# Causal widths for the single-pass score and average matmuls of an attention and feed-forward kernel

## Chip, cores and metric

The kernel runs on one core of a Trainium2 chip. The metric is device time in microseconds of one execution; the time before is the median of 3 runs.

## What is computed

Three blocks follow each other: causal attention with a decay bias, a gated feed-forward layer, and a second one that takes the maximum of three products. The shapes are B = 4, H = 8, S = 576, D = 64; 2304 tokens; widths 512 to 2048 to 512, then 512 to 768 (three times) to 512.

```python
scores = scale * q @ k.T                          # per batch and head, 576 x 576
cum = cumsum(max(s, 0)); bias = -(cum[:, None] - cum[None, :])
scores = where(causal, -1e9, scores + min(bias, 0))
attn = exp(scores - scores.max()); attn = attn / (attn.sum() + 1e-9)
x = attn @ v                                      # heads side by side: 2304 x 512
h = x @ w_in;  x = (h * clip(h + 3, 0, 6) / 6) @ w_out
h = max(max(x @ w1, x @ w2), x @ w3);  out = h @ w_out2
```

## The kernel before

**A list scheduler writes the order.** The kernel's Python code is a set of generators ("threads"). Each yields either an event, a buffer from a stock, or a request for an engine with a cost in microseconds, as `yield "PE", 2 * mm(n - z)`. The class Flow (L111 to L196) plays these out in modelled time: an engine that is free takes the request of the lowest rank, and the instruction is issued right behind the yield. So the order on each engine, and that of the DMAs, all issued on SyncE's queue, follows from the costs. The cost of a matmul of n columns is `mm(n) = n / 2400 + 0.003` (L199). At run time each engine follows its list in order, and semaphores do the rest.

**Precision.** Float32 operands are split into a rounded high part and the rest, both of the type fp32r; a product is then three single-pass matmuls (high by high, high by low, low by high; `three`, L448 to L452). Batch 0 differs: its averages, and the scores of its first pair of heads, run on plain float32 operands in four passes, which the trace shows as two records for each instruction.

**Attention.** A head's 576 queries come in 5 chunks (c = 0 to 4, the last with 64 queries). `slot` (L764) does one chunk: scores into a PSUM bank, two matmuls for each part (the second one carries the rows of the bias, 66 of them), then the masked minimum on VectorE (L800), exp on ScalarE (L808), the scaling by 1/sum on GpSimd (L346), transposes by TensorE (L849), and a copy of the transposed chunk into a tile et (high part by ScalarE, low part by VectorE, L858). Causality asks for w = (c + 1) * 128 key columns; chunk 4 takes its 576 in two parts of 288. L773 takes `max(w, 256)`, so chunk 0 computes 256 columns where it needs 128; what lies behind w is never read.

`average` (L864) multiplies the transposed weights by the values. A head's chunks form two groups: g = 0 holds queries 0 to 255 and key blocks 0 and 1, g = 1 queries 256 to 575 and key blocks 0 to 4. For batches 1 to 3, each key block x takes two matmuls (high and low part of the weights) whose stationary operand holds both parts of the values side by side (128 columns). L887 sets the first query column: 0 for x up to 2, otherwise n - 256. So key block 1 of group 0 has 256 columns, and key blocks 3 and 4 of group 1 have 256 of 320. Of these, the query columns that lie ahead of the key block are zero. `real_et` (L538) makes the two fp32r tiles for batches 1 to 3 when batch 0 has left the space, and fills these blocks with zeros once (L552, L554, L555), on GpSimd, since no later instruction writes there.

**The feed-forward layers** fill TensorE between the attention's pieces. `hidden1` and `reduce1` run the first layer in two rounds (z = 0 with 6 of 16 column blocks beside the attention, z = 1 behind it), 288 tokens at a time, as 288-column triples. Then `form` (L1099) makes linear combinations of the last layers' weights for a seven-product scheme and stores 10 of 12 in DRAM, `hidden2` computes the three products and their maximum, and `reduce2` the last product. `form` takes its buffers from the stock W of 12: one for the raw weights, then, after decoding, four more (three where it shares one).

Of the kernel before, what the change touches and what calls it, by code (L numbers as in the profile page):

```python
# [198 lines left out]
def mm(n):  # L199
    return n / 2400.0 + 0.003  # L200
# [60 lines left out]
def attn_moe_moe2(ctx, tc, q, k, v, s, w_in, w_out, w1, w2, w3, w_out2, out):  # L261
# [9 lines left out]
    def stock(items=()):  # L271
        return Stock(flow, items)
# [265 lines left out]
    def real_et():  # L538
        yield heads[0, NPAIR - 1, 1].full[1]
        for item, to in lent:  # L540
            if to is DIAG:
                to.move(item, GT)
        DIAG.move((ap, "up0"), UP)
        for g in range(2):
            yield ET[g].get()
            yield ET[g].get()
            shape = [P, 2, 2, 256] if g == 0 else [P, 2, NCH, 320]
            et[1, g] = t = ap.tile(shape, F32R, tag=f"e{g + 1}", name=f"e{g + 1}", bufs=1)
            flat = t.bitcast(F32)
            yield "POOL", 0.5  # L550
            if g == 0:
                pool.memset(flat[:, :, 1, 0:128], 0.0)  # L552
            else:
                pool.memset(flat[:, :, 3, 64:128], 0.0)  # L554
                pool.memset(flat[:, :, 4, 64:256], 0.0)  # L555
            ET[g] = stock([0])
            et_real[g].set()

# [205 lines left out]
    def slot(i, item, tiny):  # L764
        b, p, j, c = seq[i]
        h, pr = heads[b, p, j], pair[b, p]
        passes = yield h.ready
        n = min(P, S - c * P)
        qs = slice(c * P, c * P + n)
        w = min(S, (c + 1) * P)  # L770
        wp = (w + P - 1) // P * P
        e = et[0, "e4"] if c == NCH - 1 else make(item, [P, 512], F32, "e")
        cuts = [(0, 288), (288, 576)] if w > 512 else [(0, max(w, 256))]  # L773
        parts = []
        for lo, hi in cuts:
            bank = yield S_.get()
            ps = make(bank, [P, 512], F32, "ps_s")
            o = ps[:n, 0:hi - lo]
            if (b, p) == (0, 0):
                yield "PE", len(passes) * 4 * mm(min(hi, w) - lo), False, i - AHEAD  # L780
                o, hi = ps[:n, 0:min(hi, w) - lo], min(hi, w)
            else:
                yield "PE", 2 * mm(hi - lo), False, i - AHEAD
            for x, (lhs, rhs) in enumerate(passes):
                pe.matmul(  # L785
                    o, lhsT=lhs[:, qs], rhs=rhs[:, lo:hi],
                    start=(x == 0), stop=(x == len(passes) - 1),
                )
            parts.append((bank, ps, lo, min(hi, w)))
        h.scored += 1  # L790
        if h.scored == NCH:
            for st, it in h.release:
                st.put(it)
        small = make((ap, f"tiny{tiny}"), [P, 4], F32, "tiny")
        m0 = 3.0e38
        shift = (NCH - 1 - c) * P
        for x, (bank, ps, lo, hi) in enumerate(parts):
            m = small[:n, x:x + 1]
            yield "DVE", dve2(hi - lo)
            vec.tensor_tensor_reduce(  # L800
                out=e[:n, lo:hi], in0=ps[:n, 0:hi - lo], in1=above[:n, shift + lo:shift + hi],
                scale=-0.125, scalar=m0, op0=ALU.add, op1=ALU.min, accum_out=m,
            )
            S_.put(bank)
            m0 = m
        r = small[:n, 2:3]
        yield "ACT", act1(w) + 0.186
        act.activation(  # L808
            e[:n, :w], e[:n, :w], AF.Exp, bias=m0, scale=-1.0, accum_out=r,
        )  # L810
        yield "DVE", 0.07
        vec.tensor_scalar(out=r, in0=r, scalar1=1e-9, scalar2=None, op0=ALU.add)
        yield "DVE", 0.075
        vec.reciprocal(r, r)  # L814
        spread = b == 0 and c in DIAGC
        if spread:
            z = yield DIAG.get()
            diag = make(z, [P, P], F32, "diag")
            e_ = yield [(x, COST["scale"][x](P)) for x in ON["diag"]]
            if e_ == "ACT":  # L820
                act.activation(diag[:n, :n], ident[:n, :n], AF.Copy, scale=r)
            else:
                (pool if e_ == "POOL" else vec).tensor_scalar(
                    out=diag[:n, :n], in0=ident[:n, :n], scalar1=r, scalar2=1.0,
                    op0=ALU.mult, op1=ALU.mult,
                )
        else:
            yield from scaled(e[:n, :w], r, w, ON["norm", b == 0])
        TINY.put(tiny)
        g = 0 if c < 2 else 1  # L830
        if b > 0:
            yield et_real[g]
        if c in (0, 2):
            x = yield ET[g].get()
            h.et[g] = (x, et[min(b, 1), g])
            h.claimed[g].set()
        else:
            yield h.claimed[g]
        x, dst = h.et[g]
        o = (c if g == 0 else c - 2) * P  # L840
        bank = yield T.get()
        pt = make(bank, [P, c + 1, n], F32, "pt")
        yield "PE", (4 if spread else 2) * mm(n) * (c + 1)
        for y in range(c + 1):
            cut = e[:n, y * P:(y + 1) * P]
            if spread:
                pe.matmul(pt[:, y, :], lhsT=cut, rhs=diag[:n, :n], start=True, stop=True)
            else:
                pe.transpose(pt[:, y, :], cut, ident[:n, :n])  # L849
        if spread:  # L850
            DIAG.put(z)
        (E4 if c == NCH - 1 else E).put(item)
        dh = dst[:, x, 0:c + 1, o:o + n]
        yield from drained(dh, pt, n * (c + 1), ON["eh", b == 0])
        if b > 0:
            dl = dst[:, 1, 0:c + 1, o:o + n]
            yield "DVE", dve2(n * (c + 1))
            vec.tensor_tensor(out=dl, in0=pt, in1=dh.bitcast(F32), op=ALU.subtract)  # L858
        T.put(bank)
        h.count[g] += 1  # L860
        if h.count[g] == (2 if g == 0 else 3):
            h.full[g].set()

    def average(b, p, j, g):  # L864
        h, pr = heads[b, p, j], pair[b, p]
        if (j, g) == (0, 0):
            xi = yield X32.get()
            pr.x32.set((make(xi, [P, S], F32, "x32"), xi))
        x32, _ = yield pr.x32
        yield h.full[g]  # L870
        vhl = yield h.v
        nj, o, n = GROUP[g]
        y, src = h.et[g]
        bank = yield V.get()
        px = make(bank, [P, 512], F32, "px")
        xo = x32[j * D:(j + 1) * D, o:o + n]
        for x in range(nj):
            last = x == nj - 1
            if b == 0:
                z = max(0, x * P - o)  # L880
                yield "PE", 4 * mm(n - z), not last
                pe.matmul(
                    px[0:D, z:n], lhsT=vhl[:, x, j], rhs=src[:, y, x, z:n],
                    start=(x == 0), stop=last,
                )
            else:
                z = n - 256 if x > 2 else 0  # L887
                yield "PE", 2 * mm(n - z), not last
                for hl in range(2):
                    pe.matmul(  # L890
                        px[:, z:n], lhsT=vhl[:, x, j].rearrange("p l d -> p (l d)"),
                        rhs=src[:, hl, x, z:n], start=(x + hl == 0),
                        stop=(last and hl == 1),
                    )
        ET[g].put(y)
        pr.used += 1
        if pr.used == 4:
            pr.vrelease[0].put(pr.vrelease[1])
        if b == 0:
            yield from drained(xo, px[0:D, 0:n], n, ON["xo"])  # L900
        else:
            ui = yield UP.get()
            up = make(ui, [D, 320], F32, "up")
            yield from drained(up[:, 0:n], px[D:P, 0:n], n, ON["up"])
            yield "DVE", dve2(n)
            vec.tensor_tensor(out=xo, in0=px[0:D, 0:n], in1=up[:, 0:n], op=ALU.add)
            UP.put(ui)
        V.put(bank)
        pr.count += 1
        if pr.count == 4:  # L910
            pr.done.set()
# [180 lines left out]
    def forms_by_name(n, made, single):  # L1092
# [3 lines left out]
            "11": t3[:, 0], "12": t3[:, 1], "22": single,  # L1096
        }

    def form(n):  # L1099
        ri = yield W.get()  # L1100
        r = make(ri, [P, 2, 512], F32R, "wr")
        for half in range(2):
# [7 lines left out]
        if n == 1:  # L1110
            spare, both = yield shared
        else:
            spare = yield W.get()
            both = make(spare, [P, 2, 2, HK], F32R, "wg")
            if n == 0:
                shared.set((spare, both))
        single = both[:, n % 2]
        am = yield AM.get()
        y = make(am[0], [P, HK], F32, "ws")
# [555 lines left out]
```

## Time and profile before

| | |
|---|---|
| time, median of 3 runs | 948.64 us (944.84 to 956.93) |
| profiled execution, span from first to last instruction | 947.3 us |
| TensorE busy in it | 912.1 us, 6460 matmuls |
| up to 125 us: TensorE busy, granted clock | 102.7 us of 125, 0.80 |
| 125 to 350 us | 218.0 us of 225, 0.99 |
| 350 to 666 us | 315.6 us of 316, 1.00 |
| 666 to 947 us | 275.8 us of 281, 1.00 |

How to read it: the trace has one record for each instruction and engine. TensorE has two rows, PE for the matmuls and PEld for the loads of their stationary operand; both overlap among neighbours, since matmuls are pipelined and their ends are modelled, so the cost of one is read from the distance between two starts and not from its length. A form such as `128*64 128x288` means 128 rows by 64 weight columns, and 128 rows by 288 streamed columns. The granted clock is the share of TensorE's full speed that the throttle let through; 1.00 is its level of 2.4 GHz, 0.5 that of 1.2 GHz. A bracket at a row's end is the engine's idle time ahead of it and who ended it.

### The profile page before, as it was taken

What the parts mean: (1) busy time and instruction counts of PE and PEld (TensorE: products, weight loads), DVE (VectorE), ACT (ScalarE), POOL (GpSimd) and SP (SyncE); (2) the same over time, 40 slices, a digit from 0 to 9 for tenths busy, and PEclk for the clock granted to TensorE, in tenths of its full rate; (3) what the DMA queues carried; (4) which work ended last, traced back from release to release, by engine and by line L of the source; (5) the groups of instructions that cost most, each with busy time, mean ns of one, the idle gap of its engine ahead of it and who ended that gap; (6) DMA issues with size and microseconds to landing.
All of it is one profiled execution on the core that took longest, in us unless ns stands there. A gap on an engine that the chain in (4) does not pass through costs nothing.

```text
span 947.3 us, 19211 instructions
## 1 busy us (share of the span) xinstructions
PE 912.1 (96%) x6460; PEld 855.2 (90%) x6460; DVE 738.8 (78%) x2126; ACT 483.3 (51%) x1225; POOL 240.7 (25%) x323
## 2 busy tenths in 40 slices
PE   9887789999999999999999999999999999999998
PEld 5454379988999999999999999999999999999998
DVE  5788779898988943999687889896757666677994
ACT  3575458786887754566444445454223232333552
POOL 4776667666765432310000000000000000000000
PEclk7798779999999999999999999999999999999999
DMA  5799678688876424666449758978762130283542
GB/s 178 170 241 238 177 201 207 186 231 215 213 203 182 125 89 158 201 200 208 129 133 341 272 191 293 308 263 277 275 203 63 39 88 26 75 309 98 158 147 75
DMA packets 97273, 174.96 MB, mean 185 GB/s; under 512 B 10620, under 2 KB 59772, under 8 KB 97176
## 3 DMA queue, kind: packets, MB, share of 16 engines
q1 hardware_dynamic: 97176, 173.75, 60.7%
q8 instruction: 51, 0.84, 0.4%
q14 instruction: 46, 0.38, 0.1%
HBM read 97.99 MB, written 49.17 MB: 155 GB/s over the span
## 4 chain that ended last, share of the span: by engine, by line
PE 73%; DMA 10%; DVE 7%; issue 5%; ACT 2%; POOL 2%; SPq 1%; DVEq 0%; POOLq 0%; ACTq 0%
PE ps_j L451 7%; PE ps_j L452 7%; PE ps_j L450 7%; PE ps_x L452 6%; PE ps_x L450 6%; PE ps_x L451 6%; PE ps_h L450 5%; PE ps_h L451 5%; PE ps_h L452 5%; PE ps_s L785 5%; DMA raw<-in_w_out_dram 3%; PE pt L849 3%; PE px L890 3%; DMA kt<-kb 3%; PE ps_o L451 2%
## 5 line engine op out<-in xcount | busy, mean ns | idle before, releaser
L450 PE MATMUL ps_h<-x,w 128*128 128x288 f32 x512 | 153.3, 299 | 0.0
L450 PE MATMUL ps_x<-gt,w 128*128 128x288 f32 x512 | 151.8, 296 | 0.1
L452 PE MATMUL ps_x<-gt,w 128*128 128x288 f32 x512 | 151.4, 296 | 0.0
L451 PE MATMUL ps_h<-x,w 128*128 128x288 f32 x512 | 151.1, 295 | 0.0
L451 PE MATMUL ps_x<-gt,w 128*128 128x288 f32 x512 | 150.6, 294 | 0.2
L452 PE MATMUL ps_h<-x,w 128*128 128x288 f32 x512 | 150.7, 294 | 0.0
L451 PE MATMUL ps_j<-xf,wf 128*128 128x288 f32 x432 | 127.9, 296 | 0.0
L452 PE MATMUL ps_j<-xf,wf 128*128 128x288 f32 x432 | 127.7, 296 | 0.0
L450 PE MATMUL ps_j<-xf,wf 128*128 128x288 f32 x432 | 127.6, 295 | 0.0
L346 POOL TENSOR_SCALAR e<-e,tiny 128x256 f32<-128x256 f32 (+4 forms) x152 | 101.5, 672 | 82.4 <-DVE tiny L814 25.3
L808 ACT ACTIVATE e<-e,tiny 128x128 f32<-128x128 f32 (+4 forms) x160 | 95.9, 600 | 35.5 <-DVE tiny L800 24.5
L978 ACT ACTIVATE u<-ps_h,half 128x288 f32<-128x288 f32 x128 | 63.6, 497 | 81.4 <-PE ps_h L452 80.6
L785 PE MATMUL ps_s<-kt,qt 66*64 66x288 f32 (+11 forms) x384 | 100.3, 360 | 2.7 <-DVE tiny L800 1.8
L450 PEld LDWEIGHTS ps_x<-gt,w 128*128 128x128 f32 x512 | 96.1, 188 | 1.2 <-DVE g L982 0.4
L450 PEld LDWEIGHTS ps_h<-x,w 128*128 128x128 f32 x512 | 96.1, 188 | 1.0
L451 PEld LDWEIGHTS ps_x<-gt,w 128*128 128x128 f32 x512 | 96.2, 188 | 0.8 <-POOL gt L352 0.7
L452 PEld LDWEIGHTS ps_x<-gt,w 128*128 128x128 f32 x512 | 96.2, 188 | 0.4 <-DVE w L352 0.4
L451 PEld LDWEIGHTS ps_h<-x,w 128*128 128x128 f32 x512 | 96.4, 188 | 0.2
L452 PEld LDWEIGHTS ps_h<-x,w 128*128 128x128 f32 x512 | 96.2, 188 | 0.0
L800 DVE CUSTOM_DVE_ANT_0 e<-ps_s,above 128x128 f32<-128x128 f32 (+4 forms) x160 | 75.0, 474 | 21.6 <-PE ps_s L785 19.7
L849 PE MATMUL pt<-ident,e 128*128 128x128 f32 (+1 forms) x472 | 72.7, 278 | 19.2 <-POOL e L346 13.9
L982 DVE SCALAR_TENSOR_TENSOR g<-u,ps_h 128x288 f32<-128x288 f32 x128 | 57.5, 449 | 41.9 <-ACT u L978 40.9
(160 smaller groups left out, 2169.0 us busy)
## 6 DMA issues: line engine op xcount, KB each, us to landing
x<-x_d SPq DMA_DIRECT2D x64, 288.0 KB
f_d<-wf SPq DMA_DIRECT2D x30, 512.0 KB
wf<-f_d SPq DMA_DIRECT2D x30, 512.0 KB
kt<-kb SPq DMA_DIRECT2D x90, 144.0 KB
raw<-in_w_out_dram SPq DMA_DIRECT2D x22, 512.0 KB
x_d<-xs SPq DMA_DIRECT2D x16, 576.0 KB
raw<-in_w_dram SPq DMA_DIRECT2D x18, 512.0 KB
qt<-qb SPq DMA_DIRECT2D x30, 288.0 KB
```

Source lines behind the costliest of these rows:

```text
L346: (pool if e == "POOL" else vec).tensor_scalar(out=y, in0=y, scalar1=r, scalar2=1.0, op0=ALU.mult, op1=ALU.mult)
L450: pe.matmul(ps, lhsT=wh, rhs=xh, start=first, stop=False, skip_group_check=again)
L451: pe.matmul(ps, lhsT=wh, rhs=xl, start=False, stop=False, skip_group_check=again)
L452: pe.matmul(ps, lhsT=wl, rhs=xh, start=False, stop=last, skip_group_check=again)
L785: pe.matmul(o, lhsT=lhs[:, qs], rhs=rhs[:, lo:hi], start=(x == 0), stop=(x == len(passes) - 1),)
L800: vec.tensor_tensor_reduce(out=e[:n, lo:hi], in0=ps[:n, 0:hi - lo], in1=above[:n, shift + lo:shift + hi], scale=-0.125, scalar=m0, op0=ALU ...
L808: act.activation(e[:n, :w], e[:n, :w], AF.Exp, bias=m0, scale=-1.0, accum_out=r,)
L849: pe.transpose(pt[:, y, :], cut, ident[:n, :n])
L890: pe.matmul(px[:, z:n], lhsT=vhl[:, x, j].rearrange("p l d -> p (l d)"), rhs=src[:, hl, x, z:n], start=(x + hl == 0), stop=(last and hl == 1),
L978: act.activation(ut, ps, AF.Relu, bias=half, scale=1.0 / 6.0)
L982: vec.scalar_tensor_tensor(out=g, in0=ut, scalar=1.0, in1=ps, op0=ALU.min, op1=ALU.mult)
```

## The change

Chunk 0 of the scores computes 128 columns, not 256, for all heads whose scores are single-pass (the first pair had that already). The averages of batches 1 to 3 start at the first query column of their key block: `z = max(0, x * P - o)`. That makes 128 columns of key block 1 in group 0, 192 of key block 3 and 64 of key block 4 in group 1. The zero blocks are then never read, and their memsets and the cost that the scheduler was told for them go. The costs given to the scheduler follow the new widths. Beside it, a stock of three turns lets at most three threads of `form` at a time stand between their start and the moment when they have all buffers.

```diff
--- before.py
+++ after.py
@@ -546,13 +546,6 @@
             yield ET[g].get()
             shape = [P, 2, 2, 256] if g == 0 else [P, 2, NCH, 320]
             et[1, g] = t = ap.tile(shape, F32R, tag=f"e{g + 1}", name=f"e{g + 1}", bufs=1)
-            flat = t.bitcast(F32)
-            yield "POOL", 0.5
-            if g == 0:
-                pool.memset(flat[:, :, 1, 0:128], 0.0)
-            else:
-                pool.memset(flat[:, :, 3, 64:128], 0.0)
-                pool.memset(flat[:, :, 4, 64:256], 0.0)
             ET[g] = stock([0])
             et_real[g].set()
 
@@ -770,15 +763,14 @@
         w = min(S, (c + 1) * P)
         wp = (w + P - 1) // P * P
         e = et[0, "e4"] if c == NCH - 1 else make(item, [P, 512], F32, "e")
-        cuts = [(0, 288), (288, 576)] if w > 512 else [(0, max(w, 256))]
+        cuts = [(0, 288), (288, 576)] if w > 512 else [(0, w)]
         parts = []
         for lo, hi in cuts:
             bank = yield S_.get()
             ps = make(bank, [P, 512], F32, "ps_s")
             o = ps[:n, 0:hi - lo]
             if (b, p) == (0, 0):
-                yield "PE", len(passes) * 4 * mm(min(hi, w) - lo), False, i - AHEAD
-                o, hi = ps[:n, 0:min(hi, w) - lo], min(hi, w)
+                yield "PE", len(passes) * 4 * mm(hi - lo), False, i - AHEAD
             else:
                 yield "PE", 2 * mm(hi - lo), False, i - AHEAD
             for x, (lhs, rhs) in enumerate(passes):
@@ -786,7 +778,7 @@
                     o, lhsT=lhs[:, qs], rhs=rhs[:, lo:hi],
                     start=(x == 0), stop=(x == len(passes) - 1),
                 )
-            parts.append((bank, ps, lo, min(hi, w)))
+            parts.append((bank, ps, lo, hi))
         h.scored += 1
         if h.scored == NCH:
             for st, it in h.release:
@@ -876,15 +868,14 @@
         xo = x32[j * D:(j + 1) * D, o:o + n]
         for x in range(nj):
             last = x == nj - 1
+            z = max(0, x * P - o)
             if b == 0:
-                z = max(0, x * P - o)
                 yield "PE", 4 * mm(n - z), not last
                 pe.matmul(
                     px[0:D, z:n], lhsT=vhl[:, x, j], rhs=src[:, y, x, z:n],
                     start=(x == 0), stop=last,
                 )
             else:
-                z = n - 256 if x > 2 else 0
                 yield "PE", 2 * mm(n - z), not last
                 for hl in range(2):
                     pe.matmul(
@@ -1096,7 +1087,10 @@
             "11": t3[:, 0], "12": t3[:, 1], "22": single,
         }
 
+    FORMING = stock(range(3))
+
     def form(n):
+        turn_ = yield FORMING.get()
         ri = yield W.get()
         r = make(ri, [P, 2, 512], F32R, "wr")
         for half in range(2):
@@ -1114,6 +1108,7 @@
             both = make(spare, [P, 2, 2, HK], F32R, "wg")
             if n == 0:
                 shared.set((spare, both))
+        FORMING.put(turn_)
         single = both[:, n % 2]
         am = yield AM.get()
         y = make(am[0], [P, HK], F32, "ws")
```

## Rows read from the trace of the kernel before

**Rows 1.** The page's head: span, then busy time, share and instructions of each engine.

```profile
span 947.3 us, 19211 instructions
PE 912.1 (96%) x6460; PEld 855.2 (90%) x6460; DVE 738.8 (78%) x2126; ACT 483.3 (51%) x1225; POOL 240.7 (25%) x323
```

**Rows 2.** Windows: stretch, us, busy PE, PEld, DVE, ACT, POOL; granted clock, DMA share, GB/s.

```profile
0.00:125.00 125.00, 102.68 (x423) 60.61 (x423) 90.17 (x305) 65.12 (x170) 83.66 (x103) 0.80 0.80 203
125.00:350.00 225.00, 217.96 (x1602) 206.24 (x1603) 194.10 (x756) 167.93 (x465) 136.48 (x199) 0.99 0.69 184
350.00:666.00 316.00, 315.64 (x2375) 314.11 (x2375) 253.25 (x570) 158.76 (x351) 20.53 (x21) 1.00 0.68 229
```

**Rows 3.** Groups of TensorE's instructions by form: count, busy us, mean ns, idle before.

```profile
L890 PE MATMUL px<-e,vhl 128*128 128x256 f32 x192 | 40.3, 293 | 2.4 <-DVE x L906 1.0 <-DVE tiny L812 0.9
...
L785 PE MATMUL ps_s<-kt,qt 128*128 128x256 f32 x60 | 19.8, 331 | 1.7 <-issue 0.9 <-DVE tiny L800 0.8
```

**Rows 4.** Timeline of TensorE's matmuls: start us, length us, instruction, count.

```profile
212.27 0.40 PE L890 MATMUL px<-e,vhl 128*128 128x256 f32 x2
212.51 0.30 PE L450 MATMUL ps_x<-gt,w 128*128 128x288 f32 x1
212.64 0.29 PE L451 MATMUL ps_x<-gt,w 128*128 128x288 f32 x1
```

**Rows 5.** Weight loads: three rows of the timeline, then two groups by form.

```profile
211.05 0.39 PEld L849 LDWEIGHTS pt<-ident,e 64*128 64x128 f32 x5 [0.29 <-POOL e L346]
211.50 0.19 PEld L450 LDWEIGHTS ps_x<-gt,w 128*128 128x128 f32 x1
211.61 0.19 PEld L451 LDWEIGHTS ps_x<-gt,w 128*128 128x128 f32 x1
...
L785 PEld LDWEIGHTS ps_s<-kt,qt 66*128 66x128 f32 x120 | 23.9, 199 | 0.0
...
L785 PEld LDWEIGHTS ps_s<-kt,qt 66*64 66x64 f32 x60 | 8.7, 145 | 0.3
```

**Rows 6.** Groups of TensorE's instructions by form, from 150 to 346 us alone.

```profile
L450 PE MATMUL ps_h<-x,w 128*128 128x288 f32 x98 | 31.0, 316 | 0.0
L450 PE MATMUL ps_x<-gt,w 128*128 128x288 f32 x99 | 30.4, 307 | 0.0
...
L785 PE MATMUL ps_s<-kt,qt 128*64 128x288 f32 x40 | 12.8, 321 | 0.0
```

**Rows 7.** Timeline of TensorE: batch 0's four-pass averages, two records each.

```profile
69.79 0.54 PE L882 MATMUL px<-e2p,vf 128*64 128x192 f32 x2
70.16 0.38 PE L882 MATMUL px<-e1p,vf 128*64 128x128 f32 x2
70.38 0.28 PE L882 MATMUL px<-e2p,vf 128*64 128x64 f32 x2
```

**Rows 8.** Timeline of GpSimd around the zero fills of the larger tile.

```profile
114.45 0.55 POOL L554 MEMSET e<- 128x128 f32 x1 [5.23 <-PE px L882]
114.95 0.41 POOL L555 MEMSET e<- 128x384 f32 x1
115.34 1.95 POOL L352 TENSOR_TENSOR vhl<-vf,vhl 128x256 fp32r<-128x256 f32 x2
117.25 3.16 POOL L352 TENSOR_TENSOR xs<-x,xs 128x288 fp32r<-128x288 f32 x1
```

**Rows 9.** VectorE's casts of L339 (min/median/max ns, first and last start); then timeline rows.

```profile
L339 DVE CAST vhl<-vf x1: 494/494/494, 114.4 to 114.4; 128x640 fp32r<-128x640 f32 x1
...
115.44 1.00 DVE L339 CAST xs<-x 128x576 fp32r<-128x576 f32 x1
...
121.02 0.69 PE L849 MATMUL pt<-ident,e 128*128 128x128 f32 x2 [5.14 <-POOL e L346]
```

**Rows 10.** Last product of the forming, first load of the next stage, durations as above.

```profile
L352 DVE TENSOR_TENSOR wf<-ws,wf x36: 415/420/432, 490.2 to 651.2; 128x256 fp32r<-128x256 f32 x36
...
L450 PEld LDWEIGHTS ps_j<-xf,wf x432: 187/188/193, 666.0 to 872.8; 128*128 128x128 f32 x144
```

## The prediction

> **What bounds the kernel now.** I read the page first: TensorE is busy 96% of the span, its weight loads 90%, the next engine, VectorE, 78% [rows 1]. Those are averages over stages, so the second view is the windows. Up to 125 us TensorE is busy 102.7 of 125 us at a mean granted clock of 0.80: there the first batch's attention runs, and loads, decoding and softmax set the pace. From 125 to 350 us it is busy 218 of 225 us at 0.99, and from 350 to 666 us 315.6 of 316 us at 1.00 [rows 2]. The reader should see that from about 125 us on the kernel is one queue of matmuls with hardly a hole: a slot that gets shorter behind that point moves the end by as much, and what gets shorter ahead of it counts only if the dense part starts sooner.
>
> A busy share cannot tell what one matmul costs, because records overlap. So the third view is the timeline of TensorE, read by distances between starts. Two averages of 256 columns start at 212.27 and the next matmul at 212.51: 0.12 us each. A 288-column matmul starts at 212.51 and the next at 212.64: 0.13 us [rows 4]. At the granted clock of 1.00 (the 2.4 GHz level) 256 and 288 columns stream in 0.107 and 0.120 us; so a slot is the columns plus some 0.013 us.
>
> The fourth view is the weight loads, since each single-pass matmul here has its own. After a hole, with nothing streaming, one load starts at 211.50 and the next at 211.61: a load of 128 weight columns keeps the loader 0.11 us. The mean records say the same another way: 64 weight columns take 145 ns, 128 take 199, so 64 columns are 54 ns and 128 are 108. The five loads of 64-row transposes take 0.39 us together, at most 0.08 each [rows 5].
>
> **The change part by part.**
>
> *Which matmuls shrink.* Scores: the first query chunk goes from 256 to 128 columns. The row of 256-column scores (x60, and as many for the second pass) holds chunks 0 and 1 alike, so 60 instructions shrink. Averages: the x192 row of 256 columns [rows 3] is 24 heads by 8 instructions; per head two stay at 256, two go to 128, two to 192, two to 64. Together 204 instructions: 108 to 128 columns, 48 to 192, 48 to 64. The columns taken out are 108 x 128 + 48 x 64 + 48 x 192 = 26,112.
>
> *What a shorter matmul saves.* While one matmul streams, the next one's weights load. A slot is therefore the longer of its own columns and the next load. A full single-pass load is 0.108 us, a few ns short of the 256-column stream, so a matmul below 256 columns in front of such a load still has a slot of about 0.11: 0.01 us saved, whether it keeps 192 columns or 64. Only where the next load is short (transposes, scores of the 64-query chunk; by the 0.054 and the 0.08 some 0.06 us) does the slot follow the columns. Every first one of a pair is followed by its partner, with a full load: 102 instructions. For the 102 seconds I count what can follow. In the stretch from 150 to 346 us there are 40 narrow score pairs, that is 20 heads, beside 98 + 99 triples of the feed-forward [rows 6]: per head 5 groups of transposes and 2 narrow score pairs (short loads) against 4 wide score pairs, 7 average pairs and 10 triples, so 7 in 28, one in four. That is 25 instructions that save on the mean 0.05 us (54 of the seconds go from 0.12 to 0.06, 24 from 0.12 to 0.09, 24 from 0.12 to 0.06): 1.3 us. The other 179 save 0.01 each: 1.8 us. Together 3.1 us. About a tenth of the 204 lies ahead of the dense part (12 scores are the first batch's, and its successor's first heads start there) and is hidden by loads and softmax, which leaves **2.8 us**. The bounds: nothing, if VectorE's chain (194 busy of the 225 us) becomes the pace of that stage; and 26,112 columns at 2.4 GHz, 10.9 us, if no load binds.
>
> *The zero fills.* Two memsets of 0.55 and 0.41 us go, with a third, of the smaller buffer. Ahead of them GpSimd stood still for 5.23 us, until a four-pass average had released the buffer. TensorE later waits 5.14 us for a GpSimd scaling at 121.02, so the memsets lie on a chain that counts. But the wait doesn't go with them: the next GpSimd work, the low half of the values, needs VectorE's cast of them, which starts at 114.4 and takes 0.49; it can start at 114.94 in place of 115.34. Behind it the low half of the averages starts at 117.25 and needs the cast that runs from 115.44 to 116.44 [rows 8, 9]. So the chain moves up 0.4 us: **0.4 us**. The bounds: nothing, and 3.3 us if the new order puts that scaling in front of the averages' low half (3.16 us long with its gap).
>
> *The planner.* All instructions of all engines, DMAs among them, are issued in the order in which a list scheduler at build time sets them, and the shorter costs enter it. It prices a matmul of 128 columns at 0.056 us and one of 64 at 0.030, where I expect 0.11; over the 204 that is about 12 us of TensorE that it thinks free. The order will differ from the first 128-column score on. The trace can't show the new order. I take 0. Its bounds come from the holes that an order can close or open: in the dense part of the attention TensorE is idle 7 us of 225, ahead of it 22 us of 125 [rows 2]. I allow 7 us either way.
>
> *The limit of three on forming weights.* A fourth transform of weights may not take its buffers before one of three has them. Cost 0: the last product of the forming ends at 651 us and the stage that needs them starts at 666 [rows 10], a cover of 15 us. If the cover is gone, each us beyond it is a us on the end.
>
> **Sum.** -2.8 - 0.4 = -3.2 us on the profiled span of 947.3 us, that is 944.1. The median of the runs is 948.6, 1.3 us above that span, with runs from 944.8 to 956.9; against the median the forecast is **945.4 us**.
>
> **The rivals.**
>
> *Columns alone count.* If a load did overlap a short matmul without binding, the slot would be columns plus 0.013: 0.066 at 128, 0.093 at 192, 0.04 at 64. All 26,112 columns are saved, 10.9 us, some 10 of them in the dense part: about 938. For it speaks that loads are issued ahead of their matmuls; against it, that two full loads after a hole still stand 0.11 apart. The Trainium skill (TensorE: Matmul & The Clock Gate, Back-to-back issue gap) gives for sustained pairs of load and matmul 81 ns at 128 columns; by it the 108 would save 108 x 0.039 = 4.2 us, between these two cases. The same page (LDWEIGHTS) lets a load cost its columns over 1.2, however few columns stream, and this is the rule that speaks against the change; the trace's 0.108 us agrees with it.
>
> *Short single-pass matmuls are no longer single-pass.* The kernel keeps them at 256 or more everywhere; no row shows one below. If the engine then took four passes, the price is that of the first batch's four-pass averages: two records of 128 columns take 0.22 us (70.16 to 70.38) and two of 192 take 0.37 (69.79 to 70.16) [rows 7]. 108 x 0.10 + 48 x 0.25 = 22.8 us, 64 columns at no change. Nearly all of the averages' 16.8 and eight tenths of the scores' 6 lie in the dense part: +21 us, with the 0.4 of the zero fills about 969. It decides as soon as a 128-column slot is above 0.12. For it: the width was kept, zeros were even multiplied for it. Against it: weight load and 256 columns balance within a few ns, which is reason enough for that width. This is the rival on the other side.
>
> *The order decides.* Up to 7 us more idle time in the attention stage, about 952, or as much less, about 938.
>
> **How the numbers follow.** The forecast (loads bind, order neutral within 4 us) 0.60; columns alone 0.10; a worse order 0.11, a better one 0.07; four passes 0.12. The range reaches from the column case with a little of a better order, 937, to the worse order with the runs' spread, 955; outside are four passes and a remainder. The forecast's own range is 941 to 950. Faster by over 2% means below 929.7, slower above 967.6; 2% is about what a measurement of this kernel can tell from no change. Slower has two thirds of the four-pass case and a remainder: 0.10. Faster would need columns and order together and more: 0.03.
>
> **What would show it.** Right: starts of 128- and 64-column matmuls in front of full loads 0.11 us apart, 0.06 in front of transposes; TensorE's busy share in the attention stage about as before; the hole of GpSimd around 109 to 114.5 us ended by something other than a memset; the dense part starting within a few us of 125. Wrong: slots of 0.07 or less between full loads (columns count), or of 0.2 and over (four passes); a dense part that starts 5 us earlier or later, which would be the order; a hole on TensorE around the start of the last stages, which would be the forming.

## The result

The changed kernel takes 955.13 us, median of 20 runs (948.19 to 958.45); the kernel before 948.12 us, median of 20 (943.1 to 956.93). The ratio is 1.0059 with a 95% interval of 1.0039 to 1.0080: about 6 us slower (the medians differ by 7), where 3 us faster were forecast. It is inside the 2% and just outside the range, whose upper end is 955.

The page of the changed kernel's profile, head lines as in [rows 1]:

```profile
span 956.4 us, 19259 instructions
PE 919.9 (96%) x6460; PEld 856.8 (90%) x6460; DVE 736.0 (77%) x2125; ACT 481.3 (50%) x1217; POOL 243.7 (25%) x329
```

The span is 9.1 us longer, with as many matmuls. The shares say nothing on why. The windows of the changed kernel, to be laid beside [rows 2]:

```profile
0.00:125.00 125.00, 107.52 (x432) 63.56 (x433) 90.49 (x311) 67.88 (x176) 82.22 (x101) 0.77 0.75 205
125.00:350.00 225.00, 217.01 (x1594) 204.93 (x1593) 190.07 (x745) 162.59 (x451) 142.65 (x209) 0.98 0.70 185
350.00:666.00 316.00, 310.24 (x2304) 304.76 (x2304) 248.14 (x556) 154.30 (x338) 18.85 (x20) 1.00 0.65 216
```

The reader should look at the counts of matmuls, the first bracket of each row, which are not blurred by overlapping records. Up to 350 us 432 + 1594 = 2026 matmuls were started, before 423 + 1602 = 2025: the two kernels are level when the attention is nearly over. In the next 316 us there are 2304, not 2375: 71 fewer, and at 0.13 us each that is 9.2 us, all of the difference. So the time is lost behind the attention, in a stage whose matmuls the change hardly touches, and which had 0.4 us of holes before. The longest waits of TensorE in the changed kernel from 350 to 600 us (who waited for whom: us in total, times, longest); the kernel before has none in that stretch:

```profile
PE ps_x L450 <- ACT w L337: 1.6, 3, 0.8
PE ps_x L451 <- POOL gt L352: 1.2, 2, 0.7
PE ps_h L450 <- DVE g L973: 1.1, 1, 1.1
PE ps_x L450 <- ACT gt L337: 1.1, 2, 0.9
PE ps_x L452 <- DVE w L352: 0.2, 1, 0.2
```

The tile `w` is a block of the first layer's weights, rounded and split by ScalarE and VectorE; `g` and `gt` are the gated results of that layer. In the changed kernel the waits for `w` all lie between 425 and 475 us. That window in the kernel before, then in the changed one:

```profile
425.00:475.00 50.00, 49.86 (x371) 49.04 (x371) 41.46 (x94) 26.78 (x56) 0.00 (x0) 1.00 0.55 175
```

```profile
425.00:475.00 50.00, 47.84 (x328) 43.81 (x328) 44.65 (x101) 27.25 (x56) 0.00 (x0) 1.00 0.47 148
```

That is 43 matmuls fewer, the larger part of the 70 that are missing up to 600 us. Most of the rest is missing around the waits for `gt` and `g` (14 from 350 to 400 us, 13 from 550 to 600).

The second round (z = 1) takes ten more blocks of each of its two matrices, whose buffers lie where the attention's tiles lay; their loads begin when the attention is over. Two views tell when that is. First the averages of batches 1 to 3, in the kernel before and in the changed one (min/median/max ns, first and last start in us, forms):

```profile
L890 PE MATMUL px<-e,vhl x336: 274/290/616, 115.1 to 361.0; 128*128 128x256 f32 x96, 128*128 128x320 f32 x72
```

```profile
L881 PE MATMUL px<-e,vhl x336: 191/302/468, 115.2 to 370.0; 128*128 128x320 f32 x72, 128*128 128x256 f32 x24, 128*128 128x128 f32 x24, 128*128 128x192 f32 x24
```

Then the first load of a second-round weight on SyncE's queue, before and after:

```profile
368.73 0.89 SPq L312 DMA_DIRECT2D raw<-in_w_in_dram  x2
```

```profile
377.09 0.89 SPq L312 DMA_DIRECT2D raw<-in_w_in_dram  x2
```

The last average comes 9 us later, the weights 8.4 us later. In TensorE's list, 735 matmuls of the fill (396 `ps_h`, 339 `ps_x`) stand ahead of the last average before, 807 (432 and 375) in the changed kernel: 72 more, 9.4 us at 0.13. That led to the theory that was tested: **the new prices give a new order, in which the attention's tail comes later; the second round's weights follow as late, and TensorE runs dry.** The rivals: the narrow matmuls themselves cost time, and the limit of three costs time.

**What the narrow matmuls cost.** Timeline of the changed kernel, TensorE (start us, length us, instruction, count), two places: narrow scores and narrow averages in front of triples of the fill:

```profile
203.80 0.34 PE L777 MATMUL ps_s<-kt,qt 128*128 128x128 f32 x2
203.97 0.34 PE L450 MATMUL ps_x<-gt,w 128*128 128x288 f32 x1
204.15 0.29 PE L451 MATMUL ps_x<-gt,w 128*128 128x288 f32 x1
...
216.49 0.30 PE L881 MATMUL px<-e,vhl 128*128 128x64 f32 x2
216.63 0.38 PE L450 MATMUL ps_h<-x,w 128*128 128x288 f32 x1
216.85 0.30 PE L451 MATMUL ps_h<-x,w 128*128 128x288 f32 x1
```

and the weight loads there:

```profile
203.91 0.19 PEld L450 LDWEIGHTS ps_x<-gt,w 128*128 128x128 f32 x1
204.02 0.19 PEld L451 LDWEIGHTS ps_x<-gt,w 128*128 128x128 f32 x1
...
216.61 0.19 PEld L450 LDWEIGHTS ps_h<-x,w 128*128 128x128 f32 x1
216.72 0.19 PEld L451 LDWEIGHTS ps_h<-x,w 128*128 128x128 f32 x1
```

The starts of the matmul records mislead here: the two narrow averages and the triple's first matmul seem to follow within 0.07 us each (216.49 to 216.63). But the triple's second matmul starts at 216.85, so 0.36 us hold two narrow slots and one of 0.13: 0.115 for a matmul of 64 columns. In the twelve other places where the trace shows two such averages right in front of a triple, it is 0.35 to 0.36 as well. With 128 columns, 203.80 to 204.15, it is 0.11. The loads stand 0.11 apart, as they did after a hole [rows 5]. A matmul that has too few columns to cover the next load waits for it, and 64 columns cost as much as 128. What a narrow matmul costs in front of a short load, 0.06 us in the prediction, was not read from the trace.

### The profile page after: what moved, and what is told of

The parts are those of the page before. It is cut to its first block, busy times and chain, and to the rows that moved or that the text cites. A ratio compares the mean times of both kernels' runs of the same rounds, so it can differ in the third digit from the quotient of the medians.

```text
span 956.4 us, 19259 instructions
## 1 busy us (share of the span) xinstructions
PE 919.9 (96%) x6460; PEld 856.8 (90%) x6460; DVE 736.0 (77%) x2125; ACT 481.3 (50%) x1217; POOL 243.7 (25%) x329
## 4 chain that ended last, share of the span: by engine, by line
PE 79%; DMA 6%; DVE 5%; issue 4%; POOL 3%; SPq 1%; ACT 1%; POOLq 0%; DVEq 0%; ACTq 0%
PE ps_j L451 7%; PE ps_j L452 7%; PE ps_j L450 7%; PE ps_x L450 6%; PE ps_s L777 6%; PE ps_x L452 6%; PE ps_h L450 6%; PE ps_h L451 6%; PE ps_h L452 6%; PE ps_x L451 6%; PE pt L841 4%; PE px L881 3%; PE px L874 2%; PE ps_o L451 2%; PE ps_o L452 2%
## 5 line engine op out<-in xcount | busy, mean ns | idle before, releaser
L346 POOL TENSOR_SCALAR e<-e,tiny 64x576 f32<-64x576 f32 (+4 forms) x152 | 104.1, 689 | 78.7 <-DVE tiny L806 35.0
L777 PE MATMUL ps_s<-kt,qt 66*64 66x288 f32 (+13 forms) x384 | 101.6, 366 | 2.5 <-DVE tiny L792 2.4
```

What stands on the lines that cost most here:

```text
L346: (pool if e == "POOL" else vec).tensor_scalar(out=y, in0=y, scalar1=r, scalar2=1.0, op0=ALU.mult, op1=ALU.mult)
L777: pe.matmul(o, lhsT=lhs[:, qs], rhs=rhs[:, lo:hi], start=(x == 0), stop=(x == len(passes) - 1),)
```

## Experiments

Each was timed beside the kernel before; the ratio is to its runs. "Place of the last average" is counted in TensorE's list, against the kernel before.

**1. Narrow matmuls alone.** The costs told to the scheduler stay as they were, so every engine's list is that of before but for the memsets.

```diff
-            flat = t.bitcast(F32)
             yield "POOL", 0.5
-            if g == 0:
-                pool.memset(flat[:, :, 1, 0:128], 0.0)
-            else:
-                pool.memset(flat[:, :, 3, 64:128], 0.0)
-                pool.memset(flat[:, :, 4, 64:256], 0.0)
...
                 yield "PE", 2 * mm(hi - lo), False, i - AHEAD
+                o, hi = ps[:n, 0:min(hi, w) - lo], min(hi, w)
...
                 yield "PE", 2 * mm(n - z), not last
+                z = max(0, x * P - o)
```

> The narrow matmuls alone: widths of the changed kernel, zero fills gone, but the scheduler is told the old costs, so every engine's list is in the order of before and the limit of three is not there. Theory 'order' (the slowdown comes from the new order, narrow matmuls save 0.01 us each in front of a full load): 2 to 4 us faster than before, ratio 0.996 to 0.998, slots of 0.11 us, end of the attention's last average at about 359 us. Rival 'width' (the narrow matmuls themselves cost, by the granted clock falling in the attention stage): 5 to 7 us slower, ratio about 1.006, with stretches at a granted clock of 0.5 behind 130 us. Rival 'forming' (the limit of three costs): as theory 'order' here.

Measured: 946.46 us, ratio 0.9975 (0.9953 to 0.9996), 2.4 us faster. The averages end at 361.2 us (before 361.0). Narrow matmuls are worth what the loads leave of them, and don't cost time. One stretch at a lower granted clock showed up here too (last section). Of the zero fills nothing reaches TensorE. GpSimd now waits for VectorE's cast and starts its next work 0.6 us behind the cast's start, before 0.9 [rows 8, 9]. But that work takes 2.33 us, not 1.95, so that from the cast's start to the transposes for which TensorE waits it is 6.6 us in both kernels. All of it comes half a microsecond later here, since the cast waited for an average; TensorE waits 5.49 us where it waited 5.14.

```profile
114.92 0.49 DVE L339 CAST vhl<-vf 128x640 fp32r<-128x640 f32 x1 [0.42 <-PE px L877]
...
115.50 2.33 POOL L352 TENSOR_TENSOR vhl<-vf,vhl 128x256 fp32r<-128x256 f32 x2 [6.07 <-DVE tiny L807]
...
121.57 0.90 PE L844 MATMUL pt<-ident,e 128*128 128x128 f32 x3 [5.49 <-POOL e L346]
```

**2. The new order alone.** Lists of the changed kernel, widths of before, zero fills kept without a cost.

```diff
+            flat = t.bitcast(F32)
+            if g == 0:
+                pool.memset(flat[:, :, 1, 0:128], 0.0)
+            else:
+                pool.memset(flat[:, :, 3, 64:128], 0.0)
+                pool.memset(flat[:, :, 4, 64:256], 0.0)
...
                 yield "PE", 2 * mm(hi - lo), False, i - AHEAD
+                o = ps[:n, 0:max(hi - lo, 256)]
...
                 yield "PE", 2 * mm(n - z), not last
+                z = n - 256 if x > 2 else 0
```

> The new order alone: every list in the order of the changed kernel, its limit of three too, but the matmuls are 256 columns wide as before and the zero fills are there (three memsets, now without a cost in the scheduler). Theory 'order': 7 to 10 us slower than before, ratio 1.007 to 1.010, since it lacks the 3 us of the narrow matmuls. Rival 'width': no slower than before, ratio 0.998 to 1.002. Rival 'forming': about 1.006.

Measured: 956.07 us, ratio 1.0067 (1.0040 to 1.0094). With the widths and fills of before, the new lists alone give all of the slowdown. The windows from 350 to 600 us of experiment 1, then of this one:

```profile
350.00:600.00 250.00, 249.75 (x1878) 248.06 (x1877) 200.28 (x438) 125.06 (x271) 20.53 (x21) 1.00 0.65 216
```

```profile
350.00:600.00 250.00, 243.33 (x1794) 237.40 (x1794) 194.42 (x426) 123.24 (x264) 17.87 (x19) 1.00 0.61 202
```

84 matmuls fewer in 250 us (17 of them were done earlier, up to 350 us), with wide matmuls as with narrow ones.

**3. The limit of three alone**, on the kernel before (its lines as in the change's diff).

> The limit of three alone, on the kernel before. Lists agree with before up to the forming stage, behind it some differ. Theory 'order' (the attention's tail does it): no difference, ratio 0.998 to 1.002. Rival 'forming': 5 to 7 us slower, ratio about 1.006, with holes of TensorE behind 470 us.

Measured: 947.68 us, ratio 0.9985 (0.9966 to 1.0004), 1875 matmuls between 350 and 600 us as before. In the order of before the limit costs nothing.

**4. The changed kernel with an earlier tail.** In the order before and in the changed one, the averages of the last two heads have ranks of 160 to 167, the fill 159 and 160: TensorE gives them a place only where no fill is at hand. The cap puts them in front of it.

```diff
-                    flow.start(i + BEHIND + 2 * g, average(b, p, j, g))
+                    flow.start(min(i + BEHIND + 2 * g, 150 + g), average(b, p, j, g))
```

> The changed kernel with one line more: the averages' rank is capped at 150 + g, so that the last heads' averages are not outranked by the feed-forward's fill (rank 159). Theory 'order, by the tail': in the changed kernel 72 more fill matmuls stand ahead of the last average than before, so the attention ends 9 us later, the second round's weights are loaded 9 us later, and TensorE runs dry between 350 and 600 us. With the cap the last average comes at about 350 us, not 370, the second round's first weight load before 362 us, the holes of 350 to 600 us shrink from about 9 to under 3 us, and the time falls by 6 to 9 us: ratio to before 0.995 to 1.000. If the tail is not the cause, the ratio stays at 1.004 to 1.008 and the holes stay.

Measured: 941.04 us, ratio 0.9923 (0.9897 to 0.9950); the fastest of all, 14 us under the changed kernel. The place of the last average is 75 ahead; the averages end at 341.3 us, and from 350 to 600 us no hole is left:

```profile
350.00:600.00 250.00, 249.93 (x1891) 249.70 (x1891) 208.34 (x454) 124.83 (x274) 16.52 (x16) 1.00 0.67 224
```

It is faster than before by more than the tail explains: up to 350 us it started 466 + 1634 = 2100 matmuls, 75 more. A cap changes the whole order, and this one happens to be better in its first 125 us (466 to 423) as well.

**5. A later tail, and nothing else.** Experiment 1 again, with the averages of the last four heads put off (the expectation says three; `i >= 140` takes in four). The list is that of before for its first 1665 matmuls.

```diff
-                    flow.start(i + BEHIND + 2 * g, average(b, p, j, g))
+                    flow.start(i + BEHIND + 2 * g + (10 if i >= 140 else 0), average(b, p, j, g))
```

> Narrow matmuls in the order of before (as the run with the old order), with one edit that puts off the attention's tail: averages of the last three heads get a rank higher by 10. TensorE's list is that of before for its first 1665 matmuls, then the last average stands 78 places later. Theory 'the attention's tail': it ends 8 to 10 us later than in the old order (near 370 us, not 361), the second round's weights come as much later, holes of 5 to 9 us open on TensorE between 350 and 600 us, and the time goes to 952 to 956 us, ratio 1.003 to 1.008. Rival 'other parts of the new order' (its first 125 us or the middle of the attention made the changed kernel slow): no holes, time as with the old order, ratio 0.996 to 0.999.

Measured: 960.99 us, ratio 1.0118 (1.0092 to 1.0144): 14 us more than without the edit, more than expected. The averages end at 369.7 us, and the waits between 350 and 600 us are those of the changed kernel, for the same tile first:

```profile
PE ps_x L450 <- ACT w L337: 4.4, 6, 1.9
PE ps_x L450 <- ACT gt L337: 1.3, 1, 1.3
PE ps_h L450 <- DMA x<-x_d: 1.2, 1, 1.2
```

1768 matmuls were started in that stretch (before 1875). This is the cleanest evidence for the mechanism: the lists of the attention's start and middle are the same, only its tail is late. Between 425 and 475 us, where all the waits for `w` are, 299 were started, 76 fewer than in experiment 1. That a late tail costs this time is shown; that most of it goes by way of the late weights is read from the waits, since no run delays the weights alone.

**6. An earlier tail in the order of before**: experiment 1 with the cap of experiment 4.

> Narrow matmuls in the old prices, with the averages' rank capped at 150 + g: the last average stands 105 places earlier than in before. Theory 'the attention's tail': in the order of before no hole is left behind 350 us that the tail could have caused, so an earlier tail gives at most 1 us over the run with the old order: ratio 0.995 to 0.998. If an earlier tail is worth time by itself (as the 8 us of the capped changed kernel could be read), the ratio falls to 0.990 or below.

Measured: 956.01 us, ratio 1.0067 (1.0040 to 1.0093). Neither case expected that. No hole above 0.2 us opens from 350 to 600 us (1888 matmuls), but a new one behind it:

```profile
600.00:700.00 100.00, 92.70 (x670) 91.56 (x669) 73.10 (x181) 39.28 (x95) 0.00 (x0) 0.97 0.73 258
```

It is where the stage of the three products begins, and it is a wait for formed weights, which [rows 10] showed ready 15 us ahead. The last product of the forming (min/median/max ns, first and last start in us):

```profile
L352 DVE TENSOR_TENSOR wf<-ws,wf x36: 411/419/424, 478.6 to 684.1; 128x256 fp32r<-128x256 f32 x36
```

TensorE's timeline there:

```profile
669.05 0.40 PE L450 MATMUL ps_j<-xf,wf 128*128 128x288 f32 x1 [1.11 <-ACT wf L337]
...
671.64 0.61 PE L452 MATMUL ps_j<-xf,wf 128*128 128x288 f32 x1 [2.06 <-DVE wf L352]
```

The forming begins 12 us earlier than before (478.6, not 490.2) and ends 33 us later (684.1, not 651.2). In the trace the last raw weight is loaded at 611 us and the last three transforms are stored at 627, 646 and 671 us, one by one. That looks as if many threads held a buffer for their raw weights, and what was left served one at a time; experiment 7 tests it.

**7. The same with the limit of three.**

> The run with old prices, narrow matmuls and the capped rank of the averages, plus the limit of three on forming weights. Without the limit that kernel lost 6.7 us in a hole where the last stages begin, waiting for formed weights (slack of about 12 us between 600 and 700 us). Theory 'the early tail lets forming threads crowd the buffers, the limit of three undoes it': the hole goes, nothing opens elsewhere, ratio 0.990 to 0.996. If the hole has another cause, it stays and the ratio is 1.004 to 1.009.

Measured: 945.45 us, ratio 0.9959 (0.9930 to 0.9988), 10 us less than experiment 6. The forming ends at 653.9 us,

```profile
L352 DVE TENSOR_TENSOR wf<-ws,wf x36: 410/418/425, 484.4 to 653.9; 128x256 fp32r<-128x256 f32 x36
```

and by the windows the hole is gone but for one wait of 1.0 us, which is not for formed weights:

```profile
600.00:700.00 100.00, 98.96 (x746) 98.64 (x746) 74.96 (x184) 41.46 (x100) 0.00 (x0) 1.00 0.77 271
```

**8. Prices of 256 columns in the changed kernel**, close to what the narrow matmuls take.

```diff
-                yield "PE", 2 * mm(hi - lo), False, i - AHEAD
+                yield "PE", 2 * mm(max(hi - lo, 256)), False, i - AHEAD
...
-                yield "PE", 2 * mm(n - z), not last
+                yield "PE", 2 * mm(max(n - z, 256)), not last
```

> The changed kernel, with the scheduler told that the narrow matmuls cost as much as 256 columns (near to what they cost on the chip, 0.11 us). Again another order: the last average stands 78 places earlier than in before. Theory 'the attention's tail': the end of the attention is early, so no holes between 350 and 600 us: ratio 0.990 to 0.998. If narrow prices as such make no difference and any new order costs, it is 1.004 to 1.008 as the changed kernel.

Measured: 954.11 us, ratio 1.0055 (1.0024 to 1.0085). The forecast by the tail failed: the tail is early (78 places in the list), and most of the loss is elsewhere.

```profile
125.00:350.00 225.00, 214.92 (x1543) 201.43 (x1542) 192.53 (x753) 164.31 (x454) 138.07 (x202) 0.96 0.68 183
```

426 + 1543 = 1969 matmuls up to 350 us, 56 fewer than before: 7 us, lost in the middle of the attention, at a lower granted clock. So truer prices did not give a better order.

**9. Both edits**, the cap and the prices of 256.

> The changed kernel with both edits: prices of 256 columns for the narrow matmuls, and the averages' rank capped at 150 + g. The last average stands 129 places earlier than in before. Theory 'the attention's tail': no holes between 350 and 600 us, ratio 0.990 to 0.997, within 0.003 of the run with the prices alone. The rest of an order, as the start of the feed-forward's fill, sets what differs.

Measured: 954.57 us, ratio 1.0055 (1.0028 to 1.0081), with 427 + 1533 = 1960 matmuls up to 350 us. The same loss in the middle, which the cap doesn't reach.

**10. Which price moves the tail: that of the averages.** Narrow matmuls, the averages' new price and the limit of three; scores and zero fills at their old prices. The last average stands 63 places later.

> Narrow matmuls; of the new prices only that of the averages, with the limit of three; scores and zero fills keep their old prices. At build time the last average stands 63 places later than in before (in the changed kernel 72). Theory 'late attention, late weights': holes of 6 to 10 us between 350 and 600 us, the second round's first weight load after 374 us, ratio 1.003 to 1.008. If the averages' price is not the one that matters, 0.996 to 0.999.

Measured: 955.56 us, ratio 1.0074 (1.0047 to 1.0101), last average at 366.9 us, and the hole of the changed kernel:

```profile
350.00:600.00 250.00, 243.58 (x1787) 238.26 (x1786) 193.20 (x423) 120.42 (x261) 18.04 (x19) 0.99 0.61 203
```

**11 and 12. The scores' new price alone, with the limit of three and without.** The last average stands 78 places earlier.

> Narrow matmuls; of the new prices only that of the scores, with the limit of three. The last average stands 78 places earlier than in before. Theory: no holes between 350 and 600 us and none where the last stages begin; what is left is the middle of the attention, whose holes the order sets anew: ratio 0.988 to 0.998 if it is like before, up to 1.006 if it has the 11 us more that the kernel with prices of 256 columns has between 125 and 350 us.

> The same without the limit of three. Theory 'early tail crowds the forming': a hole of 8 to 12 us where the last stages begin, as in the capped kernel without the limit; 6 to 11 us slower than the same prices with the limit. If the limit does nothing, the two are equal within 2 us.

Measured: with the limit 949.09 us, ratio 0.9993 (0.9964 to 1.0022); without it 959.29 us, 1.0116 (1.0074 to 1.0158). From 600 to 700 us, first with, then without:

```profile
600.00:700.00 100.00, 99.12 (x747) 98.81 (x747) 74.98 (x183) 41.24 (x100) 0.00 (x0) 1.00 0.76 274
```

```profile
600.00:700.00 100.00, 93.74 (x689) 92.59 (x688) 75.68 (x187) 41.99 (x102) 0.00 (x0) 0.98 0.72 258
```

Without the limit the forming ends at 687.8 us, with it at 652.3. The averages' price without the limit has no run: in the scheduler's own model the threads of `form` then come to a standstill, each with some buffers and none with all. The same holds for the changed kernel, so its limit can't be taken away by itself.

All together, by where matmuls are missing (counts of the windows, from one profiled execution each):

| kernel | last average, places | us, ratio | to 350 us | 350 to 600 | 600 to 700 |
|---|---|---|---|---|---|
| before | 0 | 1 | 2025 | 1875 | 758 |
| changed | +72 | 1.0059 | 2026 | 1805 | 758 |
| 1 narrow, old order | 0 | 946.5, 0.9975 | 2026 | 1878 | 757 |
| 2 wide, new order | +72 | 956.1, 1.0067 | 2043 | 1794 | 758 |
| 3 limit alone | 0 | 947.7, 0.9985 | 2029 | 1875 | 758 |
| 4 changed, early tail | -75 | 941.0, 0.9923 | 2100 | 1891 | 749 |
| 5 old order, late tail | +78 | 961.0, 1.0118 | 2043 | 1768 | 758 |
| 6 early tail, no limit | -105 | 956.0, 1.0067 | 2057 | 1888 | 670 |
| 7 early tail, limit | -105 | 945.5, 0.9959 | 2008 | 1894 | 746 |
| 8 prices of 256 | -78 | 954.1, 1.0055 | 1969 | 1868 | 744 |
| 9 those, early tail | -129 | 954.6, 1.0055 | 1960 | 1871 | 747 |
| 10 averages' price | +63 | 955.6, 1.0074 | 2043 | 1787 | 758 |
| 11 scores' price, limit | -78 | 949.1, 0.9993 | 2022 | 1892 | 747 |
| 12 scores' price, none | -78 | 959.3, 1.0116 | 2027 | 1882 | 689 |

The four kernels with a late tail, and only these, have fewer than 1850 matmuls in the middle column. The two with an early tail and no limit have the hole in the last one. The two with prices of 256 for both kinds lose in the first. For both kinds of late weights there is an experiment that takes away the cause alone or adds it alone (5 against 1; 7 against 6; 12 against 11).

## Why the prediction was wrong

**The widths: right.** Loads bind; slots are 0.11 us at 128 and 64 columns. The term was -3.2 us with the zero fills; 2.4 (0.4 to 4.5) were measured in the old order. The rivals "columns alone count" (slots of 0.04 to 0.07) and "four passes" (0.2 and over) are out. The rule of the Trainium skill that spoke against the change (TensorE: Matmul & The Clock Gate, LDWEIGHTS) holds: loads of 128 weight columns stand 0.11 us apart. The same page's 81 ns for a sustained pair at 128 columns (Back-to-back issue gap) does not hold here, where such a slot takes 110.

**The zero fills: right in kind, nothing in size.** The wait moved to the cast behind, as worked out. The term held the length of GpSimd's next work fixed at 1.95 us; it took 2.33 (experiment 1), and that uses up the 0.4. Why it is longer is not shown.

**The limit of three: right**, as far as a run can tell. It costs nothing in the order of before, and it guards something: with an early tail its absence costs 10 us (experiments 7, 11, 12). The cover of 15 us that the prediction named is real, and experiment 6 is what it looks like when it is gone.

**The planner: here it failed.** The prediction took 0 for the new order, with 7 us either way, drawn from the holes in the attention. Experiment 2 shows 6.4 us by ratio, inside those bounds; between experiment 1 and the changed kernel, both narrow, it is 8.0. The 0 was a choice without a reason, and no row could have told the sign. (The 12 us that it says the scheduler thinks free are 11 by its own slots; nothing hangs on that.) Two things were within reach, though. The range's upper end took the order at its bound from the median and little of the runs' spread, and was short by 0.1 us. And the place was wrong: the text counted idle time in the attention, because that is where orders change, and never asked what waits for the attention's end. The stage behind it had 0.4 us of holes [rows 2], and the planner's term left it out. Its weights had little to spare: they came 8 us later, and it lost 9. The prediction asked what waits next only for the one stall of the zero fills, not for the attention as a whole. Its criterion "a dense part that starts 5 us earlier or later, which would be the order" did not trigger: the dense part is on time, its other end is not.

## What to carry to other kernels

Before narrowing a matmul, set its columns against the load of the next stationary operand; below that, narrower costs the same. Where a list scheduler sets the order, changed prices are a change of the order, and its effect can be larger than that of the work: here 2.4 us of work against 941 to 961 us over the orders that other prices and ranks gave. Keep the old prices once to tell the two apart, then look for what is late: the first stage whose count of matmuls falls is where to read the waits. The list itself is known before any run, and here it shows the last average 72 places later; but an early one is no promise, as experiments 6, 8 and 9 show.

## What the runs showed of the hardware

The granted clock fell in the dense part of the attention behind some of TensorE's small holes. In the trace before, no window of 5 us from 130 us to the last products is below 1.00. In the changed kernel, two are, each shown here with the one ahead of it (columns as in [rows 2]):

```profile
205.00:210.00 5.00, 4.17 (x30) 3.71 (x29) 4.47 (x21) 4.75 (x14) 4.17 (x7) 1.00 1.05 326
210.00:215.00 5.00, 4.54 (x25) 4.45 (x26) 4.02 (x16) 2.89 (x9) 1.75 (x3) 0.66 0.62 169
240.00:245.00 5.00, 3.18 (x25) 2.83 (x24) 4.94 (x8) 1.69 (x5) 3.40 (x5) 1.00 0.77 207
245.00:250.00 5.00, 4.78 (x24) 4.59 (x25) 3.22 (x18) 3.42 (x10) 2.20 (x4) 0.66 0.82 250
```

The first row of TensorE's timeline in the last window:

```profile
245.22 0.66 PE L841 MATMUL pt<-ident,e 128*128 128x128 f32 x2 [2.04 <-DVE e L850]
```

A mean of 0.66 over 5 us is a stretch at the lower level (1.2 GHz) that takes 1.7 us of TensorE's time, each. Ahead of the second fall TensorE was busy 3.18 of 5 us, with one hole of 2.04; ahead of the first 4.17 of 5, no hole above 0.7 us. So a hole in the attention can cost more than its length. Not each one does: in experiment 3, a hole of 1.91 us ahead of 231.56 had no fall behind it, and in experiment 1 one of 1.88 us at the same place had one (granted clock 0.83 from 230 to 240 us). The wide kernel in the changed order has both falls as well (granted clock 0.83 from 205 to 215 and from 240 to 250 us), so those two do not need the narrow width. But in the order of before, neither wide kernel has a fall (before, experiment 3), and the narrow ones have one in the attention (experiments 1 and 5). With one profiled execution of each, what decides stays open. The slowdown is not in these falls: the changed kernel has started as many matmuls by 350 us as the kernel before.
